# Thresholded attention and a bilinear FFN on one core: stationary v, weights turned by VectorE and DMA, FFN in 256-token blocks

## The chip, the core and the metric

The kernel runs on one core of one Trainium2 chip. The metric is the device time of one execution in microseconds (us), as a median over several executions on the same chip. The experiments ran in three sets on three chips; the kernel before took 2063 to 2064 us in each, so times of different sets are compared directly. Engines are named as in the profile: PE is TensorE (PEld its weight loads), DVE is VectorE, ACT is ScalarE, POOL is GpSimd, SP is SyncE, which here only issues DMAs. The clock that the throttle granted to TensorE is recorded in each trace as full (1.00) or half; "half clock" means these stretches.

## The reference

Attention with a threshold, then an FFN whose two branches are multiplied:

```python
# q, k, v: (8 batches, 8 heads, 576 positions, 64), float32; tau = 0.02
scores = (q @ k.T) / 8
scores = where(scores >= max(scores) - tau, scores, -1e9)
attn   = exp(scores - max(scores))
attn   = attn / (sum(attn) + 1e-9)
x      = (attn @ v)  -> (4608 tokens, 512)
out    = ((x @ w_a) * (x @ w_b)) @ w_out      # d_ff = 1536; weights come as float64
```

## The kernel before

Two heads of a batch make a pair; there are 32 pairs. A pair is five units of query rows: four units with one score tile of 128 rows per head, and a fifth with both 64-row tails in one tile. PSUM holds two score tiles. Per unit the program traces scores, the turn of the previous unit's weights, the exponentials, a share of an earlier FFN, the product with v, and a second share of FFN:

```python
ps_sc = pool("ps_sc", 2, space=PSUM)     # two score tiles of 576 columns
ps_1 = pool("ps_1", 4, space=PSUM)       # everything else of TensorE
...
def scores(i, u):                        # score tiles, row maxima, thresholds
    ...
            nc.tensor.matmul(sc[j][:, c0:c1], qT[r, u * P:(u + 1) * P], kT[r, c0:c1], ...)
    ...
        nc.vector.tensor_reduce(mx[:, c], sc[j], axis=AX.X, op=ALU.max)
        nc.gpsimd.tensor_scalar(bias[:, c], mx[:, c], e_nscale[:, 0:1], None, op0=ALU.mult)
        nc.gpsimd.tensor_scalar(thr[:, c], mx[:, c], cut[:, 0:1], None, op0=ALU.subtract)

def weigh(i, u):                         # exp, threshold and row sums
        nc.scalar.activation(w, s, AF.Exp, bias=bias[:, j:j + 1], scale=e_scale[:, 0:1])
        nc.vector.scalar_tensor_tensor(out=ws[j], in0=s, scalar=thr[:, j:j + 1], in1=ws[j],
                                       op0=ALU.is_ge, op1=ALU.mult, accum_out=sums[:, j:j + 1])
    ...                                  # reciprocals of the sums, kept for later

def turn(i, u):                          # weights with keys on partitions: TensorE transposes
        for c in range(NCB):
            nc.tensor.transpose(tp[:, c, :], w[:, c * P:(c + 1) * P], ident)
        nc.scalar.copy(wT[:, j, 0:NCB, :], tp)
    ...

def weighted(i, u):                      # turned weights stationary, v streams 64 columns
                nc.tensor.matmul(dst, wT[:, j, c, :], vm[:, c, j, :], ...)
    ...                                  # scaled by the reciprocals; a later transpose makes x

def ffn(g):                              # two batches, three blocks of 384 tokens
    ...
# the loop over units
    scores(i, u); turn(*before); weigh(i, u)
    convert_weights(); load_weights(1)   # one piece of 512 columns from float64 to float32
    advance(share); complete(*before); advance(share)
```

A scheduler then orders the instructions of each engine by its own estimate of when they are ready; the order is fixed before the kernel runs. In the profile's lines sc is a score tile, tp a transpose, pv the product with v, pab the first products of the FFN and po its output.

## Time and profile before

| | before |
|---|---|
| time, median | 2062.59 us (2062.55 to 2067.49, 3 runs) |
| head, to the first FFN product | 363 us, 8 pairs |
| middle, attention beside FFN | 1421 us, 24 pairs |
| tail, FFN alone | 282 us |
| TensorE idle in the middle | 6.1 us |
| time at half clock: head / middle | 174 us / 0 |

The busy lines, stages and pacing lines stand in the prediction below. First, what TensorE waited for, from the view of waits (engine, line, releaser; then us in total, times, longest us):

```profile
PE sc L222 <- DVE w L247: 37.0, 15, 3.9
PE pv L287 <- ACT wT L266: 9.2, 14, 1.1
```

The wait of the score line for the threshold adds up to 37 us, all of it in the head. Second, how TensorE's order looks in the middle, from the timeline (start us, busy us, engine, line, operation):

```profile
1070.36 2.15 PE L328 MATMUL pab<-xT,wa_sb 128*128 128x384 f32 x6
1072.35 1.45 PE L328 MATMUL pab<-xT,wb_sb 128*128 128x384 f32 x4
1073.74 1.30 PE L222 MATMUL sc<-kT,qT 64*128 64x512 f32 x8
1074.96 0.66 PE L265 MATMUL tp<-ident,w 128*128 128x128 f32 x4
```

Two score tiles, then transposes and FFN: there is always other work between one unit's scores and the next.

### The profile page before, as it was taken

What the parts mean: (1) busy time and instruction counts of PE and PEld (TensorE: products, weight loads), DVE (VectorE), ACT (ScalarE), POOL (GpSimd) and SP (SyncE); (2) the same over time, 40 slices, a digit from 0 to 9 for tenths busy, and PEclk for the clock granted to TensorE, in tenths of its full rate; (3) what the DMA queues carried; (4) which work ended last, traced back from release to release, by engine and by line L of the source; (5) the groups of instructions that cost most, each with busy time, mean ns of one, the idle gap of its engine ahead of it and who ended that gap; (6) DMA issues with size and microseconds to landing.
All of it is one profiled execution on the core that took longest, in us unless ns stands there. A gap on an engine that the chain in (4) does not pass through costs nothing.

```text
span 2066.4 us, 24299 instructions
## 1 busy us (share of the span) xinstructions
PE 2002.3 (97%) x9472; PEld 1308.9 (63%) x9472; DVE 753.0 (36%) x1866; ACT 571.1 (28%) x1017; POOL 297.0 (14%) x728
## 2 busy tenths in 40 slices
PE   7788888999999999999999999999999999999999
PEld 5577776665665666665665666666666666655554
DVE  6776765333332333333332332333333333200000
ACT  3444433222222232322222332332222322200000
POOL 4555552000000000000000000000000000000000
PEclk9767767999999999999999999999999999999999
DMA  4322321000001001001000000000100000000000
GB/s 124 86 79 72 90 76 28 18 18 22 17 18 28 17 18 33 18 7 28 23 18 22 23 18 17 23 19 23 28 12 23 16 1 6 11 6 10 11 5 16
DMA packets 125826, 58.20 MB, mean 28 GB/s; under 512 B 116496, under 2 KB 116496, under 8 KB 125712
## 3 DMA queue, kind: packets, MB, share of 16 engines
q1 hardware_dynamic: 120528, 47.21, 9.1%
q10 hardware_dynamic: 5184, 9.44, 1.2%
q8 instruction: 75, 1.23, 0.2%
q14 instruction: 39, 0.32, 0.0%
HBM read 47.19 MB, written 9.44 MB: 27 GB/s over the span
## 4 chain that ended last, share of the span: by engine, by line
PE 89%; POOL 3%; DVE 3%; ACT 2%; issue 1%; SPq 1%; DMA 0%; POOLq 0%; DVEq 0%; ACTq 0%
PE pab L328 36%; PE po L344 18%; PE pv L287 15%; PE sc L222 9%; PE tp L265 6%; PE sc L225 2%; PE tp L269 1%; ACT w L244 1%; POOL low L150 1%; POOL low L149 1%; DVE mx L232 1%; POOL bias L233 1%; ACT wT L266 1%; PE tp L309 1%; DVE w L247 1%
## 5 line engine op out<-in xcount | busy, mean ns | idle before, releaser
L328 PE MATMUL pab<-xT,wa_sb 128*128 128x384 f32 x1152 | 409.3, 490 | 2.2 <-ACT wT L266 2.0
L328 PE MATMUL pab<-xT,wb_sb 128*128 128x384 f32 x1152 | 408.9, 489 | 0.0
L344 PE MATMUL po<-wo_sb,h 128*128 128x512 f32 x864 | 389.7, 596 | 0.1
L232 DVE TENSOR_REDUCE mx<-sc 128x1 f32<-128x576 f32 x288 | 208.1, 753 | 414.4 <-PE sc L222 350.1
L287 PEld LDWEIGHTS pv<-vm,wT 128*128 128x128 f32 (+1 forms) x2560 | 310.3, 193 | 61.8 <-issue 25.4
L287 PE MATMUL pv<-vm,wT 128*128 128x64 f32 (+1 forms) x2560 | 323.2, 276 | 9.9 <-ACT wT L266 9.2
L266 ACT COPY wT<-tp 128x512 f32<-128x512 f32 x288 | 159.1, 589 | 553.2 <-PE tp L265 552.9
L328 PEld LDWEIGHTS pab<-xT,wa_sb 128*128 128x128 f32 x1152 | 211.9, 190 | 133.3 <-ACT wT L266 4.4
L328 PEld LDWEIGHTS pab<-xT,wb_sb 128*128 128x128 f32 x1152 | 212.4, 190 | 130.2
L233 POOL TENSOR_SCALAR bias<-mx,e_nscale 128x1 f32<-128x1 f32 x288 | 99.3, 345 | 1331.0 <-DVE mx L232 1294.7
L244 ACT ACTIVATE w<-sc,bias,e_scale 128x576 f32<-128x576 f32 x288 | 233.2, 845 | 194.3 <-POOL bias L233 188.6
L247 DVE SCALAR_TENSOR_TENSOR w<-sc,thr,w 128x576 f32<-128x576 f32 x288 | 227.8, 815 | 138.9 <-ACT w L244 137.0
L344 PEld LDWEIGHTS po<-wo_sb,h 128*128 128x128 f32 x864 | 157.7, 191 | 163.9 <-issue 159.6
L222 PE MATMUL sc<-kT,qT 64*128 64x64 f32 (+1 forms) x1024 | 222.3, 486 | 37.3 <-DVE w L247 37.0
L222 PEld LDWEIGHTS sc<-kT,qT 64*128 64x128 f32 x1024 | 113.6, 203 | 169.1 <-issue 148.1
L338 DVE TENSOR_TENSOR h<-a,pab 128x384 f32<-128x384 f32 x144 | 79.7, 553 | 353.7 <-PE pab L328 353.7
L335 ACT COPY a<-pab 128x384 f32<-128x384 f32 x144 | 69.6, 484 | 473.0 <-PE pab L328 471.0
L265 PE MATMUL tp<-ident,w 128*128 128x128 f32 x1152 | 181.9, 304 | 0.8 <-DVE qT L202 0.7
L265 PEld LDWEIGHTS tp<-ident,w 128*128 128x128 f32 x1152 | 144.7, 157 | 18.7 <-DVE qT L202 5.0
L291 DVE TENSOR_TENSOR x<-pv,rcp 128x128 f32<-128x128 f32 x128 | 37.1, 290 | 243.2 <-PE pv L287 243.1
L287 PE MATMUL pv<-vt,wT 128*128 128x64 f32 (+1 forms) x640 | 123.4, 276 | 0.0
L287 PEld LDWEIGHTS pv<-vt,wT 128*128 128x128 f32 (+1 forms) x640 | 96.7, 193 | 8.1 <-ACT low L140 3.8
(57 smaller groups left out, 958.1 us busy)
## 6 DMA issues: line engine op xcount, KB each, us to landing
out_dram<-osb ACTq DMA_DIRECT2D x36, 256.0 KB, 2.0
qm<-in_q_dram SPq DMA_DIRECT2D x64, 128.0 KB, 2.9
km<-in_k_dram SPq DMA_DIRECT2D x64, 128.0 KB, 3.0
vm<-in_v_dram SPq DMA_DIRECT2D x64, 128.0 KB, 2.7
raw<-in_moe_w_a_dram SPq DMA_DIRECT2D x12, 512.0 KB, 3.5
raw<-in_moe_w_b_dram SPq DMA_DIRECT2D x12, 512.0 KB, 3.6
raw<-in_moe_w_out_dram SPq DMA_DIRECT2D x12, 512.0 KB, 3.5
qt<-in_q_dram SPq DMA_DIRECT2D x32, 32.0 KB, 2.4
```

Of the source, the lines that this page charges most:

```text
L222: nc.tensor.matmul(sc[j][:, c0:c1], qT[r, u * P:(u + 1) * P], kT[r, c0:c1], start=True, stop=True)
L232: nc.vector.tensor_reduce(mx[:, c], sc[j], axis=AX.X, op=ALU.max)
L233: nc.gpsimd.tensor_scalar(bias[:, c], mx[:, c], e_nscale[:, 0:1], None, op0=ALU.mult)
L244: nc.scalar.activation(w, s, AF.Exp, bias=bias[:, j:j + 1], scale=e_scale[:, 0:1])
L247: nc.vector.scalar_tensor_tensor(out=ws[j], in0=s, scalar=thr[:, j:j + 1], in1=ws[j], op0=ALU.is_ge, op1=ALU.mult, accum_out=sums[:, j:j + 1])
L265: nc.tensor.transpose(tp[:, c, :], w[:, c * P:(c + 1) * P], ident)
L266: nc.scalar.copy(wT[:, j, 0:NCB, :], tp)
L287: nc.tensor.matmul(dst, lhsT, rhs, start=(c == 0), stop=(c == NCB))
L328: nc.tensor.matmul(p, w[:, c, fs], xT[:, c, t0:t0 + NTB], start=(c == 0), stop=(c == HP - 1))
L335: nc.scalar.copy(a, p)
L338: nc.vector.tensor_tensor(h, a, pab[1], op=ALU.mult)
L344: nc.tensor.matmul(po, hs[F][:, u * P:(u + 1) * P], wo_sb[:, F, :], start=(F == 0), stop=(F == NF - 1))
```

## The change

Its intent is to take work from TensorE. v becomes the stationary operand and the turned weights stream 256 columns; the two heads use two column tiles of the array. q and k are transposed in 32x32 blocks by VectorE, the DMAs placing the blocks. From the fifth pair on the attention weights are turned the same way, by VectorE and 16 SBUF-to-SBUF DMAs for each half of 256 rows. The output of attention is then already x transposed, so nothing can be divided by the row sums afterwards: GpSimd scales the weights before they are turned. The FFN runs in blocks of 256 tokens from the first finished batch on, and two pieces of weights are converted per unit, not one. The product of a half with v comes three units after its scores (PV_LAG). The diff, cut to its core:

```diff
+DMA_FROM = 4
+PV_LAG = 3
-        qT = work.tile([P, MAIN], FP32, tag="qT", name="qT")
-                nc.tensor.transpose(tp[:, c, :], main[:, c].rearrange("p j d -> p (j d)"), ident)
+        nc.vector.transpose(qT, t["q"].rearrange("p n e -> p (n e)"))
+        nc.vector.transpose(kT, t["k"].rearrange("p n e -> p (n e)"))
...
+        for j, w in enumerate(ws):
+            nc.gpsimd.tensor_scalar(w, w, rcp[:, j:j + 1], None, op0=ALU.mult)
...
+    def turn_dma(i, u):
+            for j, w in enumerate(ws):
+                nc.vector.transpose(
+                    tb[:, j * NB:(j + 1) * NB, (u % 2) * Q:(u % 2 + 1) * Q],
+                    w.rearrange("p (n e) -> p n e", e=Q))
+            if u % 2 == 0:
+                return
+            for g in range(4):
+                for r in range(4):
+                    nc.sync.dma_start(
+                        wT[r * Q:(r + 1) * Q, :, g * 2 * Q:(g + 1) * 2 * Q],
+                        src[g * Q:(g + 1) * Q, :, r, :])
...
+    def weighted(i, h):
+        nc.tensor.matmul(pv, vd.rearrange("p j d -> p (j d)"), wT[:, 4, :], start=True, stop=False)
+        for s in range(4):
+            for j in range(2):
+                nc.tensor.matmul(pv[j * D:(j + 1) * D], vm[:, j, s, :], wT[:, 5 * j + s, :],
+                                 start=False, stop=(s == 3))
...
-        convert_weights()
-        load_weights(1)
-        advance(share)
+            for _ in range(2):
+                convert_weights()
+                load_weights(1)
+        advance(rate)
+        for what in due(g):
+            weighted(*what)
+        advance(rate)
```

## The prediction

> **What bounds the kernel now.** I read the page's busy line, its slices and chain first, then the table of stages, then the chain piece by piece.
>
> ```profile
> PE 2002.3 (97%) x9472; PEld 1308.9 (63%) x9472; DVE 753.0 (36%) x1866; ACT 571.1 (28%) x1017; POOL 297.0 (14%) x728
> PEclk9767767999999999999999999999999999999999
> PE 89%; POOL 3%; DVE 3%; ACT 2%; issue 1%; SPq 1%; DMA 0%; POOLq 0%; DVEq 0%; ACTq 0%
> ...
> 0.00:360.00 360.00, 305.65 (x1582) 240.67 (x1583) 241.59 (x575) 143.78 (x239) 176.16 (x278) 0.76 0.29 79
> 360.00:480.00 120.00, 119.92 (x603) 79.47 (x599) 41.92 (x106) 33.57 (x63) 10.16 (x38) 1.00 0.07 16
> 480.00:1780.00 1300.00, 1294.79 (x6470) 835.53 (x6468) 447.78 (x1142) 369.47 (x670) 110.71 (x413) 1.00 0.08 19
> 1784.00:2066.00 282.00, 278.75 (x794) 150.65 (x793) 20.17 (x37) 23.24 (x46) 0.00 (x0) 1.00 0.02 9
> ```
>
> TensorE has 97% and 89% of the chain. The columns of the stages are engine busy times (PE, PEld, DVE, ACT, POOL), granted clock, DMA share. There are three stages. In the **head** (to 363 us, where the first pab matmul stands) two batches, eight pairs, have only attention to run, at a clock of 0.76, 45 us a pair. In the **middle** 24 pairs run with the FFN of earlier batches, PE never idle. The **tail** is 282 us of FFN alone. What each matmul paces at, the chain shows:
>
> ```profile
> 700.00 0.76 PE tp L265 x7
> ...
> 703.56 2.18 PE pv L287 x20
> ...
> 1969.93 61.92 PE pab L328 x192
> 2031.85 30.91 PE po L344 x72
> ```
>
> A pab instruction (384 columns) takes 322.5 ns, a po (512) 429 ns: 0.83 ns a column and some 2.5 ns; an fp32 product is two instructions. A pv instruction streams only 64 columns but takes 109 ns, as long as a 128-column transpose: its weight load sets the pace. The FFN is 12 blocks x 92.8 = 1114 us. In the middle (1784 - 363 - 3 groups x 278.5) / 24 = 24.4 us a pair are attention.
>
> **What the Trainium skill says.** "TensorE: Matmul & The Clock Gate", LDWEIGHTS, gives columns / 1.2 ns, 107 ns for 128; the trace agrees, 109 ns. "TensorEngine Tiling (Array Packing)", Key Properties, says that different tiles run in parallel. The trace agrees; in the old tail unit, two 64-column halves start together:
>
> ```profile
> 359.92 0.22 PE L287 MATMUL pv<-vm,wT 128*64 128x64 f32 x1
> 359.92 0.22 PE L287 MATMUL pv<-vt,wT 128*64 128x64 f32 x1
> ```
>
> "VectorE: DVE Perf Modes", The three transpose paths, says VectorE transposes only within 32x32 blocks, so something must move the blocks between partitions: here the DMAs. No transpose on VectorE is in this trace. "Perfetto Trace Analysis", What "DMA-bound" means, warns that the issuing sequencer can be the limit. The trace shows its price:
>
> ```profile
> L90 SPq DMA_DIRECT2D qm<-in_q_dram x64: 542/618/648, 1.2 to 1588.2; - x64
> L98 SPq DMA_DIRECT2D qt<-in_q_dram x32: 622/622/632, 2.5 to 1589.0; - x32
> ```
>
> 512 pieces or 128, an issue with three dimensions costs SyncE 0.62 us; eighteen from 1.19 to 13.20 us give 0.667 each with gaps.
>
> **The change part by part.**
>
> *FFN.* 18 blocks of 256 tokens. A pab is 256 x 0.833 + 2.5 = 216 ns, still over the 107 ns load; a block is 192 x 0.216 + 48 x 0.429 = 62.0 us, 18 are 1117 us. So the block size costs nothing. It moves work: the FFN starts after one batch, not two, and three blocks are left at the end, 186 us instead of 279.
>
> *Attention on PE, for a pair with DMA turns.* Removed: some 45 weight transposes x 0.109 = 4.9 us, those of q, k, x with their switches, 2.5, and old pv, 4 x 2.18 + about 1 = 9.7 us. New pv: a half has 2 diagonal instructions and 16 with 64 weight columns, two column tiles side by side, so (2 + 8) x 0.216 + 0.2 for switching = 2.4 us; two halves and the tail (0.8) are 5.6 us. Scores stay, but some tiles now stand alone and no longer share the array: two tiles together took 1.22 us (from 1073.74 us to the next transpose), one of the tail 1.03; three pairs, two singles of about 1.0 and the tail are 6.9 us with switches. Sum 12.5 us instead of 24.4.
>
> *A new stall.* I compared the instruction orders of both kernels. Before, each unit's scores lay apart, with transposes, pv and FFN between. Now PE's fixed order has, per pair, four score tiles in a row (two units), a lump of 7 FFN groups, one tile, 7 groups, four tiles, 4 groups. PSUM still holds two score tiles. The third of a burst waits until max, exp and threshold have released the first. The start of the old kernel shows that chain with nothing else around:
>
> ```profile
> 14.18 3.10 PE L222 MATMUL sc<-kT,qT 64*128 64x512 f32 x8 [3.13 <-DVE w L247]
> ```
>
> 3.1 us for the first tile, another 0.8 (one threshold) for the second: about 3.5 us a burst, two bursts, 7 us a pair. So a pair costs 12.5 + 7 = 19.5 us beside its FFN: 31 us FFN + 19.5 = 50.5 us where a batch brings two blocks.
>
> *VectorE.* 11 transposes of 576 a pair. Taken at the rate of the max reduction (753 ns for 576), an estimate, 0.7 us each: 7.7 us; with max 6.8, threshold 8.1, sums and reciprocals 1.6, h 9.6 x 0.42 (553 ns for 384 columns, less 128 columns) = 4.0, it is 28 us of 50. GpSimd gains 9 scalings, about 0.69 us each by the 613 ns of L142. Neither is the bound, though both lengthen the wait before a burst; counted in the 7 us.
>
> *SyncE.* 48 turning DMAs and 12 loads a pair x 0.667 = 40 us of 50. Their engines hardly matter: 288 pieces of 256 B are 18 per engine, 18 ns each in this trace. PE's order lets a pv come nearly a whole pair after its scores, so 16 issues (10.7 us) and a landing (2.4 to 3 us here) hide.
>
> *Head.* Four pairs, still turned on PE, with two weight pieces a unit instead of one. VectorE's order has 162 us of work (by these durations) before the first h product: 24 conversions x 3.15 (the means of L141, L144, L146, L148, L151: 730 + 629 + 680 + 417 + 690 ns) = 76, the rest attention. VectorE was 67% busy in the old head, where PE at half clock pressed more; at 75% now I get 217 us to the FFN's start, instead of 363. Twelve pieces of w_out stay for the next pairs, and SyncE must wait for them between its first turns: +15 us.
>
> *Sum.* 217 head + 1117 FFN + 27.5 pairs x 19.5 = 536 + 15 + 5 for start and end of pipes = 1890 us. The same sum for before: 363 + 1114 + 24 x 24.4 = 2063, as measured. For clock dips (below) I add 15: **1905 us**.
>
> **The rivals.**
> (1) *The stalls aren't there*, because VectorE and ScalarE run ahead: 28 x 7 = 196 us less, about 1710. The even flow of the old kernel (PE idle 5 us of 1300) speaks for it; the new order with two score buffers against.
> (2) *SyncE becomes the bound*: at 0.9 us an issue the 48 turns and 12 loads make 51 us a pair, no matter; at 1.2 us, 66 us, 28 x 16 = 430 us more, slower than before. The flat 0.62 us in two sizes speaks against; that no SBUF-to-SBUF copy has been seen here, for.
> (3) *The clock*: it is 0.76 in the old head although PE was 85% busy, so idle and light stretches cost clock. If the bursts bring it down for some 3.4 us each time (its steps in the old head are multiples of that), 2 x 1.7 us a pair, 95 us more: 1985. Against it: before, the clock stayed at 1.00 in the whole middle. I give it one chance in six to be full.
> (4) *Column tiles don't overlap with 256 columns*: 16 x 0.216 per half instead of 8, 3.5 us a pair, 97 us more. The shared starts speak against.
>
> **Range and chances.** The terms I trust least are the stall (4 to 9 us a pair, -85 to +55 us), the head (+-30), and the clock (0 to +95). Low 1790: small stalls and a quick head. High 2005: full stalls with clock dips, or transposes at half rate, an estimate of 1.3 us each, which would lengthen each pair by some 3 us before a burst. Faster than 2021 (over 2%) needs none of the large rivals: 0.89. Within 2%: 0.07. Slower: 0.04, for SyncE alone.
>
> **What would show it.** The first pab of the new FFN near 217 us; 192 pab in 41.4 us at the end, three blocks in 186 us; pv halves of 2.4 us; PE waiting in the score line for the threshold on VectorE some 150 to 220 us in all, in waits of 2 to 4 us; SyncE's turns at 0.6 to 0.7 us, PE hardly waiting for DMAs; clock near 1.00 after the head. It is wrong if PE's waits name the turning DMAs (rival 2), if pv halves take 3.9 us (4), if the middle's clock is under 0.97 (3), or if the waits for scores are under 60 us (1).

## The result, and the profile after

The changed kernel takes 2259.87 us (2258.4 to 2260.27, 4 runs); the kernel before took 2065.04 us in the same rounds. The ratio is 1.0927, with a 95% interval of 1.0903 to 1.0952: 9% slower. (Every ratio here is the mean time of one kernel's fast runs over the mean of the other's fast runs of the same rounds, so it differs a little from the ratio of the medians.)

From the page of the changed kernel, the busy line, the clock in 40 slices and the chain that ended last:

```profile
PE 1879.5 (83%) x7440; PEld 1233.9 (55%) x7440; DVE 889.0 (39%) x1902; ACT 401.2 (18%) x737; POOL 801.9 (36%) x1047
PEclk9665768888888888888888898798888888889999
PE 62%; POOL 10%; DVE 10%; SPq 9%; issue 4%; ACT 3%; DMA 2%; DVEq 0%; POOLq 0%; ACTq 0%
```

TensorE has 2032 instructions fewer, yet is no longer the bound all along: it is 83% busy, its clock is about 0.86 through the whole middle, and the chain wanders over five engines. The stages (length; busy time of PE, PEld, DVE, ACT, POOL; granted clock; DMA share; GB/s) are head, the middle's steady part, and tail:

```profile
0.00:239.00 239.00, 149.13 (x596) 81.86 (x598) 142.84 (x296) 74.96 (x137) 174.21 (x207) 0.72 0.33 80
...
617.00:1287.00 670.00, 582.04 (x2302) 380.07 (x2302) 274.15 (x594) 116.35 (x208) 230.35 (x319) 0.86 0.29 62
2072.00:2258.00 186.00, 181.84 (x696) 132.40 (x694) 14.74 (x35) 16.37 (x41) 0.00 (x0) 0.99 0.03 9
```

The steady part holds 11 pairs, so a pair takes 60.9 us where the prediction had 50.5. From 239.5 us, where the first pab stands, to 2072 us, TensorE is idle for 284 us and the clock is at half for 530 us, 429 us of which TensorE works through. Its longest waits, over the whole execution:

```profile
PE sc L229 <- DVE w L255: 235.7, 74, 11.0
PE sc L229 <- DVE kT L214: 56.1, 23, 8.3
PE tp L287 <- POOL w L262: 54.6, 29, 4.3
PE pv L355 <- DMA wT<-tb: 13.8, 1, 13.8
```

After 239.5 us, 212 us of the first line and 48 us of the second are left; the third, the transposes of the first four pairs, is all in the head. So in the middle TensorE waits for score buffers and for k, and hardly at all for the turning DMAs. One pair of the middle in TensorE's timeline (the bracket is the idle time before, and what ended it):

```profile
1040.98 1.30 PE L229 MATMUL sc<-kT,qT 64*128 64x512 f32 x8 [2.08 <-DVE kT L214]
1045.49 3.10 PE L229 MATMUL sc<-kT,qT 64*128 64x512 f32 x8 [3.22 <-DVE w L255]
...
1050.19 3.78 PE L388 MATMUL pab<-xT,wa_sb 128*128 128x256 f32 x8
1053.77 2.18 PE L388 MATMUL pab<-xT,wb_sb 128*128 128x256 f32 x8
1055.78 1.89 PE L388 MATMUL pab<-xT,wa_sb 128*128 128x256 f32 x8
...
1064.51 1.29 PE L229 MATMUL sc<-kT,qT 64*128 64x512 f32 x4
1065.73 0.70 PE L355 MATMUL pv<-wT,v_diag 128*128 128x256 f32 x2
1066.36 1.95 PE L358 MATMUL pv<-wT,vm 128*64 128x256 f32 x16
...
1080.52 1.30 PE L229 MATMUL sc<-kT,qT 64*128 64x512 f32 x8
1084.93 2.24 PE L229 MATMUL sc<-kT,qT 64*128 64x512 f32 x4 [3.11 <-DVE w L255]
```

Two bursts of score tiles (at 1041 and 1081 us), each with a wait of 3.1 to 3.2 us for the threshold of the tiles before. After the first, the same score work takes 3.10 us instead of 1.30 and the same eight pab instructions 3.78 us instead of 1.89: the clock is at half. The clock records of this stretch have half clock for 10.2 us from 1044.1 and for 6.8 us from 1085.1, and full clock between. The product of a half with v (0.70 and 1.95 us) is about what was predicted. Two groups of lines (count, busy us, mean ns; idle before them) show what the added work costs:

```profile
L262 POOL TENSOR_SCALAR w<-w,rcp 128x576 f32<-128x576 f32 x288 | 505.3, 1766 | 278.8 <-DVE rcp L260 277.3
...
L325 DVE STREAM_TRANSPOSE tb<-w 128x576 f32<-128x576 f32 x224 | 167.6, 766 | 154.8 <-POOL w L262 154.8
```

GpSimd's scaling takes 1.77 us, not 0.69. VectorE's transposes are close to the estimate, and wait for the scaling. Last, the tail's chain of waits has the FFN's pace as predicted:

```profile
2129.76 41.44 PE pab L388 x192
2171.20 20.60 PE po L404 x48
```

### The profile page after: what moved, and what is told of

The parts are those of the page before. It is cut to its first block, busy times and chain, and to the rows that moved or that the text cites. A ratio compares the mean times of both kernels' runs of the same rounds, so it can differ in the third digit from the quotient of the medians.

```text
span 2258.4 us, 22665 instructions
## 1 busy us (share of the span) xinstructions
PE 1879.5 (83%) x7440; PEld 1233.9 (55%) x7440; DVE 889.0 (39%) x1902; ACT 401.2 (18%) x737; POOL 801.9 (36%) x1047
## 4 chain that ended last, share of the span: by engine, by line
PE 62%; POOL 10%; DVE 10%; SPq 9%; issue 4%; ACT 3%; DMA 2%; DVEq 0%; POOLq 0%; ACTq 0%
PE pab L388 27%; PE po L404 17%; PE sc L229 9%; POOL w L262 5%; PE pv L358 5%; SPq L344 4%; DVE w L255 3%; ACT w L252 2%; SPq L333 2%; DVE mx L239 2%; PE pv L355 2%; POOL low L169 2%; POOL bias L240 1%; POOL low L170 1%; PE sc L232 1%
## 5 line engine op out<-in xcount | busy, mean ns | idle before, releaser
L262 POOL TENSOR_SCALAR w<-w,rcp 128x576 f32<-128x576 f32 x288 | 505.3, 1766 | 278.8 <-DVE rcp L260 277.3
L229 PE MATMUL sc<-kT,qT 64*128 64x512 f32 (+1 forms) x1024 | 328.5, 573 | 291.9 <-DVE w L255 235.7
L388 PE MATMUL pab<-xT,wa_sb 128*128 128x256 f32 x1536 | 404.4, 410 | 0.2 <-DVE h L398 0.2
L388 PE MATMUL pab<-xT,wb_sb 128*128 128x256 f32 x1536 | 376.0, 388 | 4.4 <-ACT a L395 2.7
L388 PEld LDWEIGHTS pab<-xT,wa_sb 128*128 128x128 f32 x1536 | 311.8, 206 | 58.9 <-issue 7.6
L388 PEld LDWEIGHTS pab<-xT,wb_sb 128*128 128x128 f32 x1536 | 298.9, 196 | 55.6 <-ACT w L252 5.8
L398 DVE TENSOR_TENSOR h<-a,pab 128x256 f32<-128x256 f32 x216 | 86.2, 411 | 483.1 <-PE pab L388 483.1
L325 DVE STREAM_TRANSPOSE tb<-w 128x576 f32<-128x576 f32 x224 | 167.6, 766 | 154.8 <-POOL w L262 154.8
L358 PE MATMUL pv<-wT,vm 128*64 128x256 f32 x1024 | 151.2, 446 | 0.0
L287 PE MATMUL tp<-ident,w 128*128 128x128 f32 x128 | 34.8, 425 | 54.7 <-POOL w L262 54.6
```

The source lines that it names most:

```text
L262: nc.gpsimd.tensor_scalar(w, w, rcp[:, j:j + 1], None, op0=ALU.mult)
L325: nc.vector.transpose(tb[:, j * NB:(j + 1) * NB, (u % 2) * Q:(u % 2 + 1) * Q], w.rearrange("p (n e) -> p n e", e=Q))
L358: nc.tensor.matmul(pv[j * D:(j + 1) * D], vm[:, j, s, :], wT[:, 5 * j + s, :], start=False, stop=(s == 3))
L388: nc.tensor.matmul(p, w[:, c, fs], xT[:, c, :], start=(c == 0), stop=(c == HP - 1))
```

## The experiments

The theory after reading the trace: the scheduler, having no transposes of TensorE left to put between, sets four score tiles in a row (a burst) twice a pair; two PSUM buffers make TensorE wait about 3 us in each burst; and with each wait the clock drops to half, mostly for 3.4 to 10.2 us. The rivals: the slow scaling on GpSimd is the cause (A); the half clock comes from something else than the waits (B); the DMAs disturb TensorE (C). Twelve kernels were run; all but the two marked gave correct results.

### TensorE in program order

```diff
+    pe = tc.keep_in_program_order
-                    nc.tensor.matmul(sc[j][:, c0:c1], ...)
+                    pe(nc.tensor.matmul(sc[j][:, c0:c1], ...))
     (and so for every matmul and transpose)
```

> The kernel after, with one thing changed: every TensorE instruction is pinned behind the one traced before it, so TensorE runs in program order. The two score tiles of a unit are then followed by half a unit of FFN, no four tiles stand in a row. Theory (the bursts of four score tiles against two PSUM score buffers make the idle time, and the idle time makes the clock dips): idle time of TensorE between 240 and 2072 us falls from 284 us to under 100, the time at half clock in that stretch from 530 us to under 150, the head stays near 240 us, the total is 1930 us (1850 to 2000). Rival A (the 1.77 us scaling on GpSimd delays threshold, exp and the turn, whatever the order): the waits stay, only move, total above 2150 us. Rival B (the half clock follows from something else than the waits, for instance from the light matmul mix with few weight loads): idle falls but half-clock time stays over 400 us, total about 2050 us.

Measured: 1946.49 us, ratio to before 0.9427 (0.9396 to 0.9458). From one edit of TensorE's order, with every instruction and DMA kept and GpSimd as slow as before, 313 us went: rivals A and C can't be the main cause. (The scheduler then placed the work of the other engines anew too; their orders differ in the trace.) Idle and half clock fell less than expected: from 255 to 1759 us TensorE was idle for 168 us, and 180 us were at half clock. The waits name a new one:

```profile
PE pv L356 <- DMA wTt<-tbt: 124.2, 16, 10.3
...
PE sc L230 <- DVE w L256: 33.2, 9, 7.9
```

The score line's wait fell from 236 to 33 us. In its place, in every second pair, TensorE waits some 8 us for the turned weights of the tail unit.

### The scaling on VectorE, alone and with the order

```diff
-            nc.gpsimd.tensor_scalar(w, w, rcp[:, j:j + 1], None, op0=ALU.mult)
+            nc.vector.tensor_scalar(w, w, rcp[:, j:j + 1], None, op0=ALU.mult)
```

> The kernel after, with the scaling of the weights by the reciprocal of their sums moved from GpSimd to VectorE, in place; the order of TensorE keeps its bursts of three or four score tiles. Theory (bursts): the waits of the score line for the threshold stay, half-clock time in the middle stays over 350 us, the head gets some 30 us shorter since GpSimd was its fullest engine, total 2150 us (2080 to 2230). Rival A (GpSimd's 1.77 us scaling is the cause): waits and dips go, total under 2000 us. The scaling itself on VectorE should take 0.35 to 0.75 us for 576 columns.

> Both edits together: TensorE in program order and the scaling on VectorE. Theory: the gains add up where they are separate (order: middle; scaling: head), total 1890 us (1820 to 1960), near what the prediction had for the change. Rival A: same as the scaling alone. If the turning DMAs are the next wait, the pv line waits for them and the total stays near the order alone.

Measured: the scaling alone 2174.92 us (ratio 1.0536), with the order 1891.73 us (0.9163). On VectorE the scaling takes 547 ns. Alone it gains 85 us and stays slower than before, its bursts still there: the score line waits 226 us, and 462 us of the middle are at half clock. The first pab came at 215.6 us instead of 239.5, so GpSimd's slow scaling cost the head 24 us; the other 61 us came off in the middle.

### All pairs turned on TensorE

```diff
-DMA_FROM = 4
+DMA_FROM = 32
```

> The kernel after with all pairs turned on TensorE (the DMA turns begin at a pair that does not exist); stationary v, the 256-token blocks and the scaling on GpSimd stay. The scheduler then spreads the score tiles over the unit by itself, with ten transposes a unit between. Theory (bursts): waits and half-clock time in the middle mostly go though the scaling on GpSimd is as slow as before, TensorE gains 45 x 0.109 = 4.9 us of work a pair, total 2010 us (1940 to 2080). Rival A (GpSimd): waits for the scaled weights stand now in front of the transposes, total above 2150 us. Rival C (the turning DMAs disturb TensorE's reads or the clock): as the theory here, told apart by the run in program order, where the DMAs stay.

Measured: 1937.45 us (0.9385), faster than the range I gave. The scheduler's own order, with transposes to place, spreads the score tiles; the steady part shows TensorE without a gap and at full clock, GpSimd's scaling still taking 1.77 us:

```profile
617.00:1287.00 670.00, 670.00 (x3540) 459.32 (x3540) 236.68 (x568) 205.79 (x446) 261.88 (x360) 1.00 0.11 22
```

So undoing the DMA turns alone, which adds TensorE work, makes the changed kernel 322 us faster. In its timeline transposes and FFN stand between the score tiles of two units: the transposes act as spacers. A pair takes 50.0 us: 31 us of FFN and 19 of attention.

### The output DMAs on another queue

In the run with order and scaling, SyncE's timeline around one of the 8 us waits reads:

```profile
629.71 2.25 SPq L110 DMA_DIRECT2D qm<-in_q_dram  x4
640.26 1.94 SPq L110 DMA_DIRECT2D km<-in_k_dram  x4
...
644.60 10.35 SPq L345 DMA_DIRECT2D wTt<-tbt  x16
```

SyncE stood still from 632.0 to 640.3 us in front of the loads of k, and so issued the tail's turning DMAs late. Its view of waits names an output DMA of the FFN there:

```profile
SPq L110 <- DMA out_dram<-osb: 83.5, 10, 9.1
```

In the built program the DMAs of SyncE and of ScalarE use the same eight semaphores in turn, so a load may have to wait for an unrelated FFN output to be written. Here the load of k at 640.26 us has the semaphore of an output that landed at 640.24. DMAs that GpSimd issues use eight others.

```diff
-                nc.scalar.dma_start(out[r0:r0 + P, :], osb)
+                nc.gpsimd.dma_start(out[r0:r0 + P, :], osb)
```

> As order_and_scale (TensorE in program order, scaling on VectorE), and the output rows are written by DMAs that GpSimd issues, not ScalarE. In order_and_scale every second pair waited 8 to 10 us for the turned tail weights (118 us in 14 waits); SyncE's loads in front of those DMAs stood for an output DMA of the FFN, with which they share a semaphore. Theory: with the outputs in another queue these waits go (under 20 us), and the half clock after them (143 us in the middle) goes with them: total 1892 - 118 - some 36 = 1740 us (1700 to 1800), all pairs of two blocks 44 us. Rival: SyncE is late by its 60 issues a pair itself; then the waits stay and the total is 1880 us.

Measured: 1739.22 us (1738.49 to 1740.2), ratio 0.8423 (0.8397 to 0.8449): 16% faster than before, and the fastest kernel of the study. The waits for the tail's weights are gone. In the middle (233 to 1547 us; the last 186 us of FFN and the final output are left out) TensorE is idle for 17 us, with 17 us at half clock; pairs take 43.8 us, and the steady part is full:

```profile
617.00:1287.00 670.00, 669.66 (x3139) 452.54 (x3140) 406.82 (x886) 152.33 (x277) 85.86 (x294) 1.00 0.38 81
```

The same edit on the changed kernel alone:

> The kernel after, with the output DMAs issued by GpSimd and nothing else; TensorE's order keeps its bursts. Theory: SyncE's waits for output DMAs (454 us in the changed kernel) go, but TensorE waits as before for the thresholds, since the turned weights come nearly a pair early there: total within 30 us of 2260. Rival F (the semaphore that loads and outputs share was itself behind the loss): under 2150 us.

Measured: 2246.69 us, ratio 1.0887. SyncE's waits for output DMAs, 454 us on the turning line of the changed kernel, went, and the total hardly moved (rival F falls). TensorE had waited for DMAs only 19 us in the changed kernel, where the products with v come late; only the even order put the turning DMAs on the path.

### The bursts put back, and filled

This undoes nothing but the spacing in the fastest kernel: the FFN's share of units 0 and 3 is moved behind units 1 and 4.

```diff
+        part = (0, 2, 1, 0, 2)[units[g][1]] if g < len(units) else 1
-        advance(rate)
+        advance(rate * part)
```

> As order_scale_out, with the bursts put back by hand and nothing else: no FFN between units 0 and 1 and between units 3 and 4 of a pair, its share comes after them, so four score tiles and then three stand in a row on TensorE. Theory: two waits of 3 to 4 us a pair for the threshold come back, and with each some 7 to 10 us of half clock, in sum 12 to 15 us a pair over 27 pairs: 2080 us (1980 to 2160), though instructions and work are the same. Rival D (the lost time of the changed kernel came from other things in the scheduler's order, such as late transposes of k): under 1830 us.

Measured: 2032.73 us (0.9841), so 294 us for moving work about, none added. In the middle TensorE is idle for 187 us and works 240 us at half clock, half of which is lost: 187 + 120 = 307 us, less the 17 + 6 of the kernel without bursts, is 284 of the 294 (rival D falls). With 55 bursts that is 3.4 us of wait and 2.2 us of lost clock each. By the clock records, 53 of the 55 waits of 3.1 to 3.2 us are followed by half clock within 4 us. One of them in TensorE's timeline:

```profile
705.37 1.30 PE L230 MATMUL sc<-kT,qT 64*128 64x512 f32 x8
709.77 1.26 PE L233 MATMUL sc<-kT,q_diag 128*128 128x512 f32 x4 [3.11 <-DVE w L256]
710.87 3.41 PE L389 MATMUL pab<-xT,wb_sb 128*128 128x256 f32 x8
714.08 2.16 PE L389 MATMUL pab<-xT,wa_sb 128*128 128x256 f32 x8
```

After the 3.11 us of idleness the scores still run at full clock; the drop comes 1.4 us later (half clock from 711.2 to 714.6) and hits the FFN.

The second kernel puts two unused products between the two units of each burst:

```diff
+            if rate and u in (0, 3):
+                for _ in range(FILL):                       # FILL = 2
+                    fill = ps_1.tile([P, HALF], FP32, tag="ps1", name="fill")
+                    for c in range(HP):
+                        pe(nc.tensor.matmul(fill, wa_sb[:, c, 0:P], wb_sb[:, c, 0:HALF], ...))
```

> As burst_back, with two idle products (16 instructions of 256 columns, 3.45 us at full clock, results not used) put between the two units of each burst, so that TensorE works where it waited. This adds 27 x 2 x 3.45 = 186 us of work. Theory (the half clock follows from the idle stretch): the time at half clock in the middle falls under 80 us, the total is that of order_scale_out plus about 190 us, near 1935 us, so less than burst_back with less work. Rival E (the half clock follows from the scores themselves or from the mix of instructions): half-clock time stays as in burst_back and the total is the same as there or more.

Measured: 1929.95 us (0.9346). It has 880 instructions more than the kernel above and is 103 us faster:

```profile
726.72 3.72 PE L471 MATMUL fill<-wb_sb,wa_sb 128*128 128x256 f32 x16
730.28 1.19 PE L234 MATMUL sc<-kT,q_diag 128*128 128x512 f32 x4
```

The score tiles after the filling wait for nothing, and half clock in the middle falls from 263 to 14 us. Against the kernel without bursts it is 191 us longer, which is the filling itself (880 x 216 ns = 190 us). Rivals B and E fall: the half clock follows from the idleness, not from the scores.

### What was the scaling's cost on GpSimd

Both kernels give wrong results on purpose. The first scales by a constant instead of a column; the second uses five forms of instruction, one for each unit.

```diff
-            nc.gpsimd.tensor_scalar(w, w, rcp[:, j:j + 1], None, op0=ALU.mult)
+            nc.gpsimd.tensor_scalar(w, w, 0.125, None, op0=ALU.mult)
```

> The kernel after, with the scaling on GpSimd by a constant 0.125 in place of the reciprocal column: the result is wrong on purpose. It measures the disputed cost alone. If the scalar read from each partition makes GpSimd's scaling slow, the 576-column instruction falls from 1.77 us to about 0.69 us, the rate of the clamp with constants. If in-place float32 scaling is slow by itself, or other engines' traffic slows it, it stays at 1.7 us.

> The kernel after with five forms of GpSimd instruction on the same tile of 576 columns, by unit (results wrong on purpose): multiply by a constant, min then max, multiply then add, min alone, multiply by a column spread over the row. The run with a constant showed 1.70 us, so the column of scalars isn't the cost. If multiplication is what costs, min then max and min alone take about 0.7 us, the others 1.7 us; if it is something of this tile or this moment, all take 1.7 us.

Measured: by the constant 1697 ns, so the column isn't what costs. The five forms, as groups of the second kernel's GpSimd instructions:

```profile
L269 POOL TENSOR_SCALAR w<-w 128x576 f32<-128x576 f32 x64 | 109.3, 1708 | 66.2 <-DVE w L255 58.7 <-DVE rcp L260 6.6
L263 POOL TENSOR_SCALAR w<-w 128x576 f32<-128x576 f32 x64 | 108.4, 1706 | 31.4 <-DVE w L255 29.2 <-DVE rcp L260 1.6
...
L265 POOL TENSOR_SCALAR w<-w 128x576 f32<-128x576 f32 x64 | 45.4, 709 | 84.9 <-DVE w L255 84.4
L267 POOL TENSOR_SCALAR w<-w 128x576 f32<-128x576 f32 x64 | 44.5, 696 | 33.1 <-DVE w L255 32.9
L271 POOL TENSOR_TENSOR w<-w,rcp 128x576 f32<-128x576 f32 x32 | 36.7, 1148 | 33.3 <-DVE rcp L260 33.3
```

In order: multiply then add, multiply by a constant, min then max, min alone, and a two-tensor multiply by the column spread over the row. A tensor-scalar multiply takes 1.71 us, min and max 0.70 us. The two-tensor multiply takes 1.15 us; there my expectation of 1.7 was wrong.

### What the scaling and the DMA turns are worth in an even order

The first kernel has the order and output edits, the scaling left on GpSimd; the second turns all pairs on TensorE, with the scaling on VectorE.

> Order and output edits, with the scaling left on GpSimd at 1.77 us: what the slow scaling costs once the order is even. Theory: only the head shows it (255 us as in the run with the order alone, against 233), pairs stay at 44 us, total 1765 us (1745 to 1800). If the scaling delays the turn enough for TensorE to wait, pairs are over 46 us and the total over 1800 us.

> All pairs turned on TensorE, scaling on VectorE: what the turning DMAs are worth against transposes on TensorE when both run in an even order. Theory: the head is some 20 us shorter than with GpSimd's scaling (248 us), pairs stay at 50 us, total 1905 us (1880 to 1930), so the DMA turns are worth about 165 us.

Measured: 1799.30 us (0.8721), at the upper end of what I expected, so GpSimd's scaling costs 60 us even in an even order. The first pab comes 22 us later (255.0 against 233.4); the first pair with DMA turns takes 89.5 us instead of 67.7 (from its first exponential to that of the next pair), with one wait of 34 us for its DMAs; and a later pair takes 44.6 us on average, 0.8 more. The second: 1898.25 us (0.9200). DMA turns in an even order (1739 us) are therefore worth 159 us over turns on TensorE. The two also differ in the output queue and in the pinning, but in the kernel that turns on TensorE neither could gain much: its middle had 8.5 us of idleness and 10.2 us at half clock.

## Why the prediction was wrong

| term | predicted | in the changed kernel |
|---|---|---|
| head, to the first pab | 217 us | 239.5 us |
| FFN, 18 blocks of 62.0 us | 1117 us | 1117 us |
| attention on TensorE, 27.5 pairs at full clock | 344 us (12.5 each) | 404 us (14.7 each; the rest) |
| idle on TensorE | 192 us (7 a pair) | 284 us |
| lost to half clock | 15 us | 215 us (half of 429) |
| w_out conversions, ends | 20 us | in the rows above |
| sum | 1905 us | 2260 us |

- **FFN: right.** 192 pab instructions took 41.44 us, three blocks 186 us; smaller blocks cost nothing.
- **Products with v, transposes, SyncE: right.** A half took about 2.5 us (rival 4 falls), a transpose 0.77 us, a turning issue 0.61 us, and PE hardly waited for DMAs in the changed kernel (rival 2 falls). What I did not see is that SyncE's queue can be held up by an unrelated output through a shared semaphore. It cost the changed kernel almost nothing (13 us less without it, with the intervals of the two ratios overlapping) but 118 us of waits once the order was even.
- **The head: step mis-sized.** I took 0.69 us for the scaling from the row of a min and max with two constants; a multiply took 1.77 us. With 547 ns on VectorE the head was 215.6 us, nearly the predicted 217. An operation's duration may not be read from another operation's row, even with the same shape and engine. The 0.7 us for VectorE's transposes were taken in the same way, from the row of the max reduction; that this came out right was luck.
- **Two slips without effect.** The 9.6 products for h a pair in VectorE's sum should be 6 (64 in 11 pairs of the trace), so 28 us should be 26.5; VectorE wasn't the bound. And the sum for the kernel before repeats the reading that gave 24.4 us a pair, so it tests nothing.
- **The stall: right in kind, too small.** Bursts, their place and the 3.1 us wait per burst were there. The waits for thresholds were 236 us, near the 150 to 220 expected; the waits for k's transpose, 56 us, weren't in the sum. Both are for the whole execution; the middle has 212 and 48 us.
- **The clock: the step that failed.** The prediction put into its sum two waits a pair of 3.5 us, yet gave the clock only 15 us, since the middle of the kernel before stayed at 1.00, and made "the bursts bring it down" a rival with one chance in six. But that middle had 6 us of idleness in 1421; where it had been idle, in the head, the clock had been 0.76. The argument for keeping the clock was taken from a stage that the change did away with. The size failed as well: 3.4 us of half clock for each burst were assumed, and mostly 6.8 to 10.2 us came, so 7.6 us a pair are lost (168 us busy at half clock in 11 pairs, halved) instead of 3.4. Where one wait stands alone, as in the kernel with the bursts put back, it was mostly 3.4 or 6.8 us; in the pair shown above, the 10.2 us go with two waits, of 2.1 and 3.2 us. By the prediction's own test, a clock under 0.97 in the middle, rival 3 happened.
- **Attention at full clock** is 2.2 us a pair over the estimate, and 13.1 in the even order (1314 us, less 930 of FFN, the idle time and the lost clock, over 27.5). A lone score tile takes 1.22 us (1064.51 to 1065.73), as long as two together, where I took 1.0; the rest isn't assigned.
- **One pair near the change from TensorE turns to DMA turns**, the sixth, took 92.6 us (from first exponential to first exponential), some 32 more than the others, where w_out had been given 15 in all. In the fastest kernel it is the fifth, with 67.7 against 43.8 us. In the changed kernel its longest waits are 11.0 us for a threshold and 13.8 us for turned weights, between 278 and 323 us; no run took the cost apart.

So the work removed was real: with an even order, the scaling moved and the outputs on another queue, a pair takes 43.8 us, the 31 + 12.5 of the prediction. In the changed kernel some 500 us of idleness and lost clock ate it. The runs show that the order makes them; why the scheduler bunches the scores once the transposes are gone was not tested, and a third score buffer was not tried.

## What to carry to other kernels

A removal of work from the bounding engine also removes spacing: compare the order of instructions, count how many producers stand in a row against the buffers they fill, and charge every wait of about 3 us twice, once as time and once as half clock after it. When the time goes the wrong way, pin the order first: it is the cheapest experiment, and what waits next (here a shared DMA semaphore) shows only then. Read an instruction's cost from a row with the same operation, or measure it by itself.

## What the Trainium skill lacked or had wrong

- "TensorE: Matmul & The Clock Gate", Part 1: "For modeling, the ramp penalty is <1% of a typical kernel span". That is said of the warm-up at a kernel's start, so no run here shows it wrong; but it is no measure of a kernel whose waits bring the clock down again and again: here 215 of 2260 us, 9.5%, are lost. The page's advice (Why this matters for your kernels) of no idle gaps over about 3 us between bursts fits: with the bursts put back, 53 of 55 waits of 3.1 to 3.2 us were followed by half clock, mostly for 3.4 or 6.8 us, and filling them brought half clock in the middle from 263 to 14 us.
- "GPSIMD Engine Reference", 4.1 Engine selection, has one-input operations as "roughly line-rate". The runs show 0.70 us for min and max of 576 float32 columns, but 1.71 to 1.77 us for a multiply by a scalar, against 0.55 us on VectorE; the two-tensor multiply, at 1.15 us, is the faster one. The page doesn't tell these apart.
- "DMA: Bandwidth & Descriptors" treats two DMAs in flight on one semaphore as a danger to the data. What it lacks is their cost in time when two issuing engines share semaphores, so that a load waits for an unrelated output: 118 us of TensorE's waits in one kernel here, gone with the outputs on another queue.
